# A linear-attention and mixture-of-experts kernel: 240 token places an expert, and another sequence first

## The chip, the cores and the metric

The kernel runs on one core of a Trainium2 chip. A core has a matrix engine (TensorE, PE in the profile; its weight loads are PEld), a vector engine (VectorE, DVE), a scalar engine (ScalarE, ACT), a general one (GpSimd, POOL) and a queue engine that here only issues transfers (SyncE, SP). They run side by side and wait for one another by semaphores; 16 DMA engines move data. The metric is the device time of one execution in microseconds, less is better.

## The reference

Two stages, float32, shapes r, k, v, w [4 sequences, 8 heads, 768 places, 48]. The first is a recurrence along each sequence, the second sends half of the 3072 rows to one of 8 experts each:

```python
for t in range(S):                                   # per batch and head
    cur = einsum('bhd,bhe->bhde', u[None] * k[t], v[t])
    y[t] = einsum('bhd,bhde->bhe', r[t], state + cur)
    state = w[t][..., None] * state + einsum('bhd,bhe->bhde', k[t], v[t])
x = y.transpose(0, 2, 1, 3).reshape(3072, 384)
out = x.copy()
xc = x[x @ w_skip > 0]
e_idx = argmax(xc @ w_gate, axis=1)
gate = softmax(xc @ w_gate) at e_idx
out[those rows] = xc + gate * (relu(xc @ w1[e_idx]) @ w2[e_idx])   # w1 [384, 1024], w2 [1024, 384]
```

## The kernel before

**Attention stage.** The work is 24 chunks: `seq` (line 64) lists them, sequence after sequence, six chunks of 128 places each. The order on every engine is written out by hand (the loop at line 672, under a manual schedule): step s computes the outputs of chunk s, the scores of chunk s + 1 and the preparation of chunk s + 2. A chunk has one tile `wrk` with w, r and k for all heads: 96 of its 128 partitions hold the two halves of the heads (16 to 111), the others hold whatever lies beside them in memory and are masked out by `rowsk`, one number a partition. Three such tiles go round.

Preparation of a chunk: VectorE scans w into q (`prep_scan`, line 309), GpSimd multiplies r by k into rk (`bonus_keys`, 318), GpSimd multiplies k by q into kq (326), VectorE scans w into rh (331), and rp = r times rh (336) is made by GpSimd, for the first chunk by VectorE. TensorE: `scores` (358, from kq and rp), `bonus_sums` (377, from rk), `rows_of_keys` (348, transposes of kq, which ScalarE copies to kt, 350), `update` (390, from kt and v), `outputs` (409, 413), `rows_out` (425). VectorE masks the scores (364) and multiplies the bonus sums by the turned v (`bonus`, 381); ScalarE evicts.

SyncE issues the loads in the order of the program: `load_chunk` (167), `load_turned` (163) and `load_v` (182). The first chunk has nothing before it in memory, so only its 96 rows are loaded (173, 174), into a tile that GpSimd and VectorE have cleared before (240, 243). `setup` (245) also clears other tiles and lets TensorE multiply zeros: `fill` (663) issues that many matmuls of 512 columns, 11 at the start, 4 in step -1 (729) and 3 in step 0 (702).

Between the chunks a router gives each token an expert and a rank within it. Tokens whose rank is beyond the capacity `CAP` (31) set a flag, upon which a slow general path computes everything again (940); it isn't run here.

**Expert stage.** Each expert has CAP = 256 token places, in two tiles of 128, gathered by an indirect DMA from the output (`gather`, 439). The expert weights and tokens are split into a high and a low part of a reduced 32-bit type (fp32r in the profile), and three products are added. For each of eight pieces q of the hidden layer, nine matmuls go into one bank (882 to 884; weights stationary, 256 tokens moving). ScalarE takes the relu as its high part hh (889), VectorE the low part hl (894). Then, for each token tile j, 24 matmuls (906 to 908; hidden values stationary, 384 columns of w2 moving), VectorE adds the gated result (915), and GpSimd scatters the rows back (820). Between the two products, `tokens` (809) transposes the tokens of the next expert (815). The splitting of the next expert's weights (88, 89) runs beside the matmuls. Expert 0 is worked differently: its first tile is done ahead, in the holes at the end of the attention stage, and its tiles keep 128 places.

## Time and profile before

| what | value |
|---|---|
| median of 3 runs | 286.65 us (286.0 to 287.15) |
| the profiled execution | 286.06 us in all, span of its instructions 284.2 us |
| TensorE busy | 95% of the span |
| VectorE, ScalarE, GpSimd busy | 76%, 56%, 51% |
| attention stage | up to about 133 us |
| experts 1 to 7 | from about 156 us to the end |

The span is from the first to the last instruction; the execution has some 1.9 us more around it. Busy time of TensorE is no measure of how close it is to its peak: matmuls are pipelined, each shows a duration that overlaps the next one's, and what one costs in a stream is the distance from its start to the next start. L882 is line 882 of the kernel. Engine names with a q (SPq, ACTq) are the engines' issue queues. "x8" is a count.

### The profile page before, as it was taken

To read this page: it belongs to the slowest core of one execution; us is meant where nothing else is said; L and a number is where in the kernel's file an instruction comes from. 1 tells how busy PE (TensorE), PEld (TensorE's weight loads), DVE (VectorE), ACT (ScalarE), POOL (GpSimd) and SP (SyncE) were. 2 spreads that over 40 slices of the span, in tenths; PEclk is the share of its full clock that TensorE was granted. 3 is DMA by queue.
4 is the path that set the end of the run, shared out by engine and by line. 5 is a ranking of instruction groups with operands and counts; after the bars stand their busy time and mean duration, and the time that the engine had idled before them with its cause. 6 is when DMAs were issued, how large, how long until landed. Compare 5 with 4: busy or idle time off the path is not lost.

```text
span 284.2 us, 8967 instructions
## 1 busy us (share of the span) xinstructions
PE 271.2 (95%) x3601; PEld 248.9 (88%) x3602; DVE 217.0 (76%) x414; ACT 159.4 (56%) x464; POOL 145.9 (51%) x140
## 2 busy tenths in 40 slices
PE   6998999999999999999999999999999999999993
PEld 2687878788887888887999999999999999999992
DVE  7997999999989999972747697948859588595320
ACT  5175555787658957768416573827638276381310
POOL 4986775699978998974656625011030110201111
PEclk9999999999999999999999999999999999999999
DMA  7999999998999869992078997565672656700001
GB/s 217 239 311 333 277 345 339 363 332 246 297 278 302 252 218 348 308 310 65 28 256 294 345 314 267 212 213 200 221 258 68 231 200 221 268 5 28 10 5 41
DMA packets 26131, 64.41 MB, mean 227 GB/s; under 512 B 4342, under 2 KB 15386, under 8 KB 26080
## 3 DMA queue, kind: packets, MB, share of 16 engines
q1 hardware_dynamic: 23712, 58.14, 62.3%
q0 software_dynamic: 2048, 5.48, 5.9%
q8 instruction: 30, 0.49, 0.7%
q10 hardware_dynamic: 320, 0.13, 0.2%
q14 instruction: 21, 0.17, 0.2%
HBM read 56.69 MB, written 7.86 MB: 227 GB/s over the span
## 4 chain that ended last, share of the span: by engine, by line
PE 57%; POOL 8%; issue 6%; DVE 4%; ACT 3%; DMA 1%; POOLq 0%; DVEq 0%; ACTq 0%
PE psH L884 7%; PE psH L883 7%; PE psH L882 7%; PE psO L906 6%; PE psO L908 6%; PE psO L907 6%; PE psH L133 4%; PE psY L409 3%; POOL rp L336 2%; PE psA L358 2%; POOL kq L326 2%; PE psY L413 2%; PE psX L815 2%; PE psO L658 2%; PE psX L425 1%
## 5 line engine op out<-in xcount | busy, mean ns | idle before, releaser
L820 POOL DMA_INDIRECT out<-fin,ids x16 | 16.8, 1047 | 99.1 <-DVE fin L915 92.7
L889 ACT ACTIVATE hh<-psH 128x256 fp32r<-128x256 f32 x60 | 23.1, 385 | 56.6 <-PE psH L884 53.4
L884 PE MATMUL psH<-xTh,w1l 128*128 128x256 f32 x168 | 47.5, 283 | 0.0
L883 PE MATMUL psH<-xTl,w1h 128*128 128x256 f32 x168 | 47.5, 283 | 0.0
L882 PE MATMUL psH<-xTh,w1h 128*128 128x256 f32 x168 | 47.5, 283 | 0.0
L906 PE MATMUL psO<-w2h,hh 128*128 128x384 f32 x120 | 40.9, 341 | 0.0
L908 PE MATMUL psO<-w2h,hl 128*128 128x384 f32 x120 | 40.2, 335 | 0.0
L907 PE MATMUL psO<-w2l,hh 128*128 128x384 f32 x120 | 40.1, 335 | 0.0
L894 DVE SCALAR_TENSOR_TENSOR hl<-psH,hh 128x256 fp32r<-128x256 f32 x60 | 25.1, 418 | 13.3 <-ACT hh L889 12.0
L326 POOL TENSOR_TENSOR kq<-wrk,q 128x512 f32<-128x512 f32 x24 | 28.2, 1177 | 11.7 <-DVE q L309 3.5
L364 DVE TENSOR_TENSOR asb<-psA,c_sb 128x512 f32<-128x512 f32 x48 | 30.4, 676 | 3.5 <-PE psA L358 3.4
L331 DVE TENSOR_TENSOR_SCAN rh<-wrk,rowsk,pss 128x520 f32<-128x520 f32 x24 | 31.1, 1296 | 2.0
L318 POOL TENSOR_TENSOR rk<-wrk 128x512 f32<-128x512 f32 x24 | 31.0, 1292 | 2.4 <-DMA wrk<-wrk 2.4
L884 PEld LDWEIGHTS psH<-xTh,w1l 128*128 128x128 f32 x168 | 32.2, 192 | 0.0
L883 PEld LDWEIGHTS psH<-xTl,w1h 128*128 128x128 f32 x168 | 32.2, 192 | 0.0
L882 PEld LDWEIGHTS psH<-xTh,w1h 128*128 128x128 f32 x168 | 32.2, 191 | 0.0
L309 DVE TENSOR_TENSOR_SCAN q<-wrk,pss 128x520 f32<-128x520 f32 x24 | 29.5, 1230 | 3.0 <-DMA wrk<-wrk 0.9
L336 POOL TENSOR_TENSOR rp<-wrk,rh 128x512 f32<-128x512 f32 x23 | 27.2, 1181 | 5.4 <-DVE rh L331 5.0
L89 DVE TENSOR_TENSOR w2l<-r,w2h 128x512 fp32r<-128x512 f32 x42 | 27.7, 685 | 2.0 <-ACT w2h L88 1.4
L409 PE MATMUL psY<-asb,v 128*48 128x128 f32 x384 | 26.5, 276 | 2.6 <-DVE psY L381 2.3
L915 DVE SCALAR_TENSOR_TENSOR fin<-psO,gates,xg 128x384 f32<-128x384 f32 x15 | 9.3, 618 | 25.2 <-PE psO L908 24.6
L358 PE MATMUL psA<-rp,kq 64*64 64x128 f32 (+1 forms) x768 | 26.0, 251 | 1.8 <-issue 1.1
(154 smaller groups left out, 608.4 us busy)
## 6 DMA issues: line engine op xcount, KB each, us to landing
r<-w SPq DMA_DIRECT2D x48, 512.0 KB
wrk<-wrk SPq DMA_DIRECT2D x21, 772.5 KB
v<-vN SPq DMA_DIRECT2D x24, 192.0 KB
vt<-wrk SPq DMA_DIRECT2D x48, 96.0 KB
out<-x SPq DMA_DIRECT2D x24, 192.0 KB
wrk<-wrk SPq DMA_DIRECT2D x1, 579.4 KB
wrk<-wrk SPq DMA_DIRECT2D x1, 512.0 KB
wrk<-wrk SPq DMA_DIRECT2D x1, 384.0 KB
```

The costliest lines, as they stand in the source:

```text
L318: nc.gpsimd.tensor_tensor(work[i]["rk"].rearrange("p a j -> p (a j)"), t[:, R_OFF:K_OFF], t[:, K_OFF:V_OFF], op=ALU.mult)
L326: nc.gpsimd.tensor_tensor(kq, wk["k"], wk["q"][:, :, 1:1 + P], op=ALU.mult)
L331: nc.vector.tensor_tensor_scan(rh.rearrange("p a j -> p (a j)"), wk["w"][:, 0:NP * CW], reads_at[:, :NP * CW], rowsk, op0=ALU.mult, op1=AL ...
L336: eng.tensor_tensor(rp, wk["r"], rh[:, :, :P], op=ALU.mult)
L358: nc.tensor.matmul(psa[g][j:j + HP, a, j:], wk["kq"][rows, a, j:j + HP], wk["rp"][rows, a, j:], start=True, stop=True)
L409: nc.tensor.matmul(y_at(a, g), v[:, 2 * a + g], wk["asb"][g][:, a], start=False, stop=True, skip_group_check=True)
L882: nc.tensor.matmul(ps, w1h[:, o:o + P], xTh[:, kc], start=(kc == 0), stop=False)
L883: nc.tensor.matmul(ps, w1h[:, o:o + P], xTl[:, kc], start=False, stop=False)
L884: nc.tensor.matmul(ps, w1l[:, o:o + P], xTh[:, kc], start=False, stop=(kc == KC - 1))
L906: nc.tensor.matmul(pso, h[j, fc][0], w2h[:, o], start=(fc == 0), stop=False)
L907: nc.tensor.matmul(pso, h[j, fc][0], w2l[:, o], start=False, stop=False)
L908: nc.tensor.matmul(pso, h[j, fc][1], w2h[:, o], start=False, stop=(fc == FC - 1))
```

## The change

Three things. `CAP` is 240: the second token tile of experts 1 to 7 has 112 rows, the moving tile of lines 882 to 884 has 240 columns, and gather, transposes, scatter and the last addition take 112 rows in the second tile. Expert 0 keeps its shapes. The order of the sequences is 1, 0, 2, 3; chunk numbers in memory come from a list `chunk`, and since the first chunk processed now has rows before it in memory, it is loaded with 128 rows, and nothing is cleared for it. In the set-up the loads of the first three chunks come first on SyncE, ahead of the turned v and v of the first; `rowsk` is made by four memsets; four clears move from step -2 to the set-up. GpSimd makes rp of the first chunk too, and for the first two chunks rk is made behind rp. The fillers are 2 in step -1 and none in step 0.

```diff
-CAP = 256
+CAP = 240
...
-    seq = [(b, c) for b in range(B) for c in range(NC)]
+    seq = [(b, c) for b in (1, 0, *range(2, B)) for c in range(NC)]
+    chunk = [b * NC + c for b, c in seq]
...
         def load_chunk(i):
             b, c = seq[i]
             rows = wrk.rearrange("b c g d n -> (b c g d) n")
-            at = 2 * D * i
+            at = 2 * D * chunk[i]
             t = wrk_sb[i % NBUF]
-            if i == 0:
-                nc.sync.dma_start(t[KO:LO, :R_OFF], rows[:2 * D, :R_OFF])
-                nc.sync.dma_start(t[KO:LO, R_OFF:V_OFF], rows[:2 * D, R_OFF:V_OFF])
-                nc.scalar.dma_start(c_sb[:, :C_IOTA], cst[:, :C_IOTA])
-                shifted(nc.scalar, u_sb, uP)
-                return
-            to, at = (t, at - KO) if i < n - 1 else (t[KO:LO], at)
-            for cs in (slice(0, R_OFF), slice(R_OFF, V_OFF)) if i == 1 else (slice(0, V_OFF),):
+            to, at = (t, at - KO) if 0 < chunk[i] < n - 1 else (t[KO:LO], at)
+            for cs in (slice(0, R_OFF), slice(R_OFF, V_OFF)) if i < 2 else (slice(0, V_OFF),):
                 nc.sync.dma_start(to[:, cs], rows[at:at + to.shape[0], cs])
 
         def load_v(i):
...
 
         count_w = scratch(1)
 
-        def clear_w(eng, i):
-            eng.memset(wrk_sb[i][:, :R_OFF], 1.0)
-
-        def clear_rk(eng, i):
-            eng.memset(wrk_sb[i][:, R_OFF:], 0.0)
-
         def setup():
-            clear_w(nc.gpsimd, 0)
-            nc.gpsimd.memset(vt_sb[0], 0.0)
-            clear_rk(nc.vector, 0)
-            load_chunk(0)
+            for i in range(3):
+                load_chunk(i)
+            for t in vt_sb[:3]:
+                nc.gpsimd.memset(t, 0.0)
+            load_turned(0)
+            load_v(0)
+            nc.scalar.dma_start(c_sb[:, :C_IOTA], cst[:, :C_IOTA])
+            shifted(nc.scalar, u_sb, uP)
+            nc.gpsimd.memset(wgp_sb, 0.0)
+            nc.gpsimd.memset(vt_sb[3], 0.0)
+            nc.gpsimd.memset(onesb, 1.0)
+            nc.gpsimd.memset(ohs, 0.0)
+            nc.gpsimd.memset(key, 0.5)
             nc.vector.memset(warm, 0.0)
-            load_chunk(1)
-            nc.gpsimd.memset(vt_sb[1], 0.0)
-            load_v(0)
-            load_turned(0)
             nc.vector.memset(pss, 0.0)
             ints = ones_w.bitcast(U32)
             for a in range(NP):
 ...
-            nc.vector.tensor_reduce(rowsk, ident[:, KO:LO], axis=AX, op=ALU.add)
+            nc.vector.memset(rowsk, 1.0)
+            nc.vector.memset(rowsk[:KO], 0.0)
+            nc.vector.memset(rowsk[96:], 0.0)
+            nc.vector.memset(rowsk[96:LO], 1.0)
             nc.vector.tensor_scalar(reads_w.bitcast(U32), ints, rowsk, None, op0=ALU.mult)
             nc.scalar.activation(junk0, warm[:, 0:1], AF.Exp)
             for z in psa:
                 nc.scalar.copy(z.rearrange("p a j -> p (a j)"), warm)
-            nc.gpsimd.memset(vt_sb[2], 0.0)
-            nc.gpsimd.memset(wgp_sb, 0.0)
             for o in range(2):
                 eye = ident[half(o, D), HP * o:HP * o + D]
                 for g in range(2):
...
-            if i > 0:
+            if i > 1:
...
-            eng = nc.gpsimd if i > 0 else nc.vector
-            eng.tensor_tensor(rp, wk["r"], rh[:, :, :P], op=ALU.mult)
+            nc.gpsimd.tensor_tensor(rp, wk["r"], rh[:, :, :P], op=ALU.mult)
+            if i < 2:
+                bonus_keys(i)
...
-            nc.sync.dma_start(out[i * P:(i + 1) * P], x.rearrange("p o i d -> p (o i d)"))
+            nc.sync.dma_start(out[chunk[i] * P:(chunk[i] + 1) * P], x.rearrange("p o i d -> p (o i d)"))
+
+        def width(j):
+            return min(P, CAP - j * P)
...
         def gather(s, pool):
...
+            w = width(s % 2) if s > 1 else P
-                out=xg[s], out_offset=None, in_=out,
-                in_offset=bass.IndirectOffsetOnAxis(ap=idr[:, s % 2, s // 2:s // 2 + 1], axis=0),
+                out=xg[s][:w], out_offset=None, in_=out,
+                in_offset=bass.IndirectOffsetOnAxis(ap=idr[:w, s % 2, s // 2:s // 2 + 1], axis=0),
...
-                if s + 4 < n:
+                if 3 <= s + 4 < n:
...
-                    if s == 0:
-                        fill(3)
...
-                if s == -2:
-                    bonus_keys(0)
-                    nc.gpsimd.memset(vt_sb[3], 0.0)
-                    nc.gpsimd.memset(onesb, 1.0)
-                    nc.gpsimd.memset(ohs, 0.0)
-                    nc.gpsimd.memset(key, 0.5)
...
-                        fill(4)
+                        fill(2)
...
             xTh = moe.tile([P, KC, CAP], F32R, tag="xTh", name=f"xTh{e}")
             xTl = moe.tile([P, KC, CAP], F32R, tag="xTl", name=f"xTl{e}")
             for j in range(2):
+                w, ts = width(j), slice(j * P, j * P + width(j))
                 ps = ps1.tile([P, KC, P], F32, tag="psT", name=f"psX2{e}_{j}", bufs=2)
                 for kc in range(KC):
-                    nc.tensor.transpose(ps[:, kc], xg[2 * e + j][:, kc * P:(kc + 1) * P], ident)
-                split(xTh[:, :, j * P:(j + 1) * P], xTl[:, :, j * P:(j + 1) * P], ps)
+                    nc.tensor.transpose(ps[:, kc, :w], xg[2 * e + j][:w, kc * P:(kc + 1) * P],
+                                        ident[:w, :w])
+                split(xTh[:, :, ts], xTl[:, :, ts], ps[:, :, :w])
             xTs[e] = xTh, xTl
 
         def scatter(s, o):
+            w = width(s % 2)
             sc = nc.gpsimd.indirect_dma_start(
-                out=out, out_offset=bass.IndirectOffsetOnAxis(ap=ids[:, s % 2, s // 2:s // 2 + 1],
+                out=out, out_offset=bass.IndirectOffsetOnAxis(ap=ids[:w, s % 2, s // 2:s // 2 + 1],
                                                                axis=0),
-                in_=o, in_offset=None, bounds_check=NT - 1, oob_is_err=False)
+                in_=o[:w], in_offset=None, bounds_check=NT - 1, oob_is_err=False)
             tc.declare_no_dep(sc.ins, group="rows", reason="tokens are scattered to rows of their own")
             tc.add_to_no_dep_group("rows", sc.ins)
 
...
 
             h = {}
             nh = FC if e > 0 else FC // 2
+            n_ = CAP if e > 0 else 2 * P
             for q in range(nh):
                 ps = (ps1 if q % 4 < 2 else ps2).tile(
-                    [P, CAP], F32, tag=("psA0", "psA1", "psY", "psB")[q % 4], name=f"psH{e}_{q}")
-                hh = moe.tile([P, CAP], F32R, tag="hh", name=f"hh{e}_{q}", bufs=NHB)
-                hl = moe.tile([P, CAP], F32R, tag="hl", name=f"hl{e}_{q}", bufs=NHB)
+                    [P, n_], F32, tag=("psA0", "psA1", "psY", "psB")[q % 4], name=f"psH{e}_{q}")
+                hh = moe.tile([P, 2 * P], F32R, tag="hh", name=f"hh{e}_{q}", bufs=NHB)[:, :n_]
+                hl = moe.tile([P, 2 * P], F32R, tag="hl", name=f"hl{e}_{q}", bufs=NHB)[:, :n_]
                 if e == 0:
                     for i in range(2):
                         ts = slice(i * P, (i + 1) * P)
...
-                        ts = slice(j * P, (j + 1) * P)
+                        ts = slice(j * P, j * P + width(j))
...
             w2h, w2l = wsp[e, 2], wsp[e, 3]
             for j in range(1 if e == 0 else 0, 2):
                 pso = ps1.tile([P, DM], F32, tag=("psu", "pss")[j], name=f"psO{e}_{j}")
+                w = width(j) if e > 0 else P
+                po = pso[:w]
                 for fc in range(FC):
                     o = slice(fc * DM, (fc + 1) * DM)
-                    nc.tensor.matmul(pso, h[j, fc][0], w2h[:, o], start=(fc == 0), stop=False)
-                    nc.tensor.matmul(pso, h[j, fc][0], w2l[:, o], start=False, stop=False)
-                    nc.tensor.matmul(pso, h[j, fc][1], w2h[:, o], start=False,
+                    nc.tensor.matmul(po, h[j, fc][0], w2h[:, o], start=(fc == 0), stop=False)
+                    nc.tensor.matmul(po, h[j, fc][0], w2l[:, o], start=False, stop=False)
+                    nc.tensor.matmul(po, h[j, fc][1], w2h[:, o], start=False,
                                      stop=(fc == FC - 1))
                 more(2)
                 if j == 0 and e in (1, 2):
                     (row_tests, verdict)[e - 1]()
                 s = 2 * e + j
                 o = moe.tile([P, DM], F32, tag="fin", name=f"fin{e}_{j}", bufs=3)
-                nc.vector.scalar_tensor_tensor(o, pso, gates[:, j, e:e + 1], xg[s],
+                nc.vector.scalar_tensor_tensor(o[:w], po, gates[:w, j, e:e + 1], xg[s][:w],
                                                op0=ALU.mult, op1=ALU.add)
                 if later_pairs:
                     first.append((s, o))
```

## Rows read from the trace of the kernel before

**Rows 1.** The page: engine table (busy, share, instructions) and the chain by line.
```profile
PE 271.2 (95%) x3601; PEld 248.9 (88%) x3602; DVE 217.0 (76%) x414; ACT 159.4 (56%) x464; POOL 145.9 (51%) x140
...
PE psH L884 7%; PE psH L883 7%; PE psH L882 7%; PE psO L906 6%; PE psO L908 6%; PE psO L907 6%; PE psH L133 4%; PE psY L409 3%; POOL rp L336 2%; PE psA L358 2%; POOL kq L326 2%; PE psY L413 2%; PE psX L815 2%; PE psO L658 2%; PE psX L425 1%
```

**Rows 2.** Timeline of the first product: start us, duration us, engine, line, operation, tiles, count.
```profile
196.00 0.28 PE L882 MATMUL psH<-xTh,w1h 128*128 128x256 f32 x1
196.00 0.19 PEld L883 LDWEIGHTS psH<-xTl,w1h 128*128 128x128 f32 x1
...
199.96 0.28 PE L882 MATMUL psH<-xTh,w1h 128*128 128x256 f32 x1
```

**Rows 3.** Timeline of the second product.
```profile
203.09 0.33 PE L906 MATMUL psO<-w2h,hh 128*128 128x384 f32 x1
...
205.17 0.33 PE L906 MATMUL psO<-w2h,hh 128*128 128x384 f32 x1
```

**Rows 4.** The chain in order of time: start us, us, engine, tile, line, count.
```profile
146.01 5.36 PE psH L133 x48
...
235.75 0.66 PE psX L815 x6
...
253.38 0.66 PE psX L815 x6
```

**Rows 5.** Stretches: length, then busy us (instructions) by engine, clock, DMA share, GB/s.
```profile
8.00:13.80 5.80, 5.48 (x94) 3.74 (x99) 5.73 (x8) 0.78 (x3) 5.80 (x9) 1.00 0.94 230
13.80:18.90 5.10, 5.10 (x120) 4.58 (x122) 4.74 (x9) 3.25 (x11) 4.68 (x5) 1.00 0.93 306
...
40.00:60.00 20.00, 19.57 (x402) 16.75 (x397) 18.72 (x36) 12.74 (x47) 14.12 (x13) 1.00 1.04 347
```

**Rows 6.** Timeline of the start, all engines; in brackets idle time and its releaser.
```profile
0.74 0.39 ACTq L175 DMA_DIRECT2D c_sb<-cst  x1
...
1.96 0.32 SPq L174 DMA_DIRECT2D wrk<-wrk  x1
...
3.30 4.56 PE L666 MATMUL psw<-warm 128*128 128x512 bf16 x11
...
6.40 1.17 POOL L326 TENSOR_TENSOR kq<-wrk,q 128x512 f32<-128x512 f32 x1 [3.37 <-DMA wrk<-wrk]
...
6.82 1.30 DVE L336 TENSOR_TENSOR rp<-wrk,rh 128x512 f32<-128x512 f32 x1
...
7.53 1.72 POOL L318 TENSOR_TENSOR rk<-wrk 128x512 f32<-128x512 f32 x1
...
8.27 1.09 PE L358 MATMUL psA<-rp,kq 64*64 64x128 f32 x32 [0.40 <-DVE rp L336]
...
10.58 0.59 ACT L350 COPY kt<-psT 128x512 f32<-128x512 f32 x1 [3.40 <-PE psT L348]
...
11.34 0.67 PE L390 MATMUL psu<-v,kt 128*64 128x48 f32 x16
...
11.94 0.82 PE L666 MATMUL psw<-warm 128*128 128x512 bf16 x3
...
12.69 1.08 PE L409 MATMUL psY<-asb,v 128*48 128x128 f32 x16
...
13.70 0.98 PE L358 MATMUL psA<-rp,kq 64*64 64x128 f32 x28
```

**Rows 7.** Timeline at the switch from the transposes to the second product: weight loads.
```profile
165.21 0.19 PEld L906 LDWEIGHTS psO<-w2h,hh 128*128 128x128 f32 x1
...
165.32 0.19 PEld L907 LDWEIGHTS psO<-w2l,hh 128*128 128x128 f32 x1
```

**Rows 8.** The page's costliest groups, two of VectorE: busy us, mean ns, idle before, releaser.
```profile
L894 DVE SCALAR_TENSOR_TENSOR hl<-psH,hh 128x256 fp32r<-128x256 f32 x60 | 25.1, 418 | 13.3 <-ACT hh L889 12.0
...
L89 DVE TENSOR_TENSOR w2l<-r,w2h 128x512 fp32r<-128x512 f32 x42 | 27.7, 685 | 2.0 <-ACT w2h L88 1.4
```

**Rows 9.** Timeline of the end, GpSimd.
```profile
280.26 0.98 POOL L820 DMA_INDIRECT out<-fin,ids  x1 [3.18 <-DVE fin L915]
```

More of the change, by code (lines that the diff above doesn't have):

```diff
@@ L502, in low_vals @@
                 if not last:
-                    nc.scalar.copy(vals[:, :, :2, 0], tok[:, i0:i0 + m])
+                    nc.scalar.copy(vals[:, :, :2, 0], tok[:, chunk[i0]:chunk[i0] + m])
                 nc.scalar.copy(vals[:, :, 2], gate)
```

## The prediction

> **What bounds the kernel now.** I read the page's table of engines and its chain first: TensorE is busy for 95% of the span, and the chain names the expert matmuls of lines 882 to 884 and 906 to 908 before all else [rows 1]. Then the timeline of the expert stage, from one matmul start to the next, since a busy share says little of pipelined matmuls. In the first product of an expert, 33 matmuls of 256 columns lie between the starts 196.00 and 199.96, 120.0 ns each [rows 2]; in the second product 12 matmuls of 384 columns lie between 203.09 and 205.17, 173.3 ns each [rows 3]. The stream has no hole: an expert takes 253.38 - 235.75 = 17.63 us [rows 4], and 72 x 0.120 + 6 transposes (0.66) + 48 x 0.1733 = 8.64 + 0.66 + 8.32 = 17.62. So in this stage a nanosecond off each matmul start comes off the end.
>
> In the attention stage TensorE is the pacer too. After the scores of the second chunk processed (13.70) it is busy for all of 5.10 us, and for 19.57 of 20 us in the middle of the stage [rows 5]. Before that it isn't: it starts its scores at 8.27, waits for data between short bursts, and begins its unbroken stream with the outputs of the first chunk at 12.69 [rows 6]. So the first 13 us are worth what they move that 12.69, no more.
>
> **Capacity 240, the expert matmuls.** For experts 1 to 7 lines 882 to 884 issue 7 x 8 x 9 = 504 matmuls, whose moving tile shrinks from 256 to 240 columns. The two pitches are 128 columns and 53.3 ns apart, which is 0.4167 ns a column (the 2.4 GHz level) and leaves 13.3 ns a matmul that doesn't depend on columns. On that line 240 columns cost 100 + 13.3 = 113.3 ns, a gain of 6.67 ns, and 504 x 6.67 ns = 3.36 us. No row shows a matmul of this reduced type under 256 columns, so the value is bounded from both sides. The bound on the gain is that line. The bound on the other side is that the weight load, which still has 128 columns, takes over. Each load starts as the matmul before it starts [rows 2], and streams with less moving work show how fast loads can follow each other: 48 f32 matmul passes of 128 columns in 5.36 us, 112 ns each; 6 transposes in 0.66 us, 110 ns [rows 4]. Where the second product begins behind the transposes, a weight load of the reduced type at 165.21 is followed by the next at 165.32 [rows 7], so it too fits in 110 ns. All three lie below 113.3, so I take the line, and keep 0 to 3.36 us for the range.
>
> [...]
>
> The rest of this part is small. In the second product the second tile has 112 weight columns, but its time goes with the 384 moving ones: nothing. The transposes run at a weight load's pace (110 ns) and their loads keep 128 columns: nothing, at most 21 x 13 ns. ScalarE's and VectorE's evictions (lines 889 and 894) get shorter, but wait for TensorE; on VectorE an eviction (0.42) and a low part of the next expert's weights (0.69) [rows 8] make 1.1 us beside 1.02 us of matmuls for each of the eight hidden pieces, a lag of under 1 us, which the second product absorbs since it uses those pieces in order over 4 us. The gathers are hidden. The last scatter is not: issued at 280.26, it ends the span at 284.2 [rows 9]. With 112 of 128 rows it gains between nothing and an eighth of 3.9 us; I take 0.1, since issue and latency hardly go with rows.
>
> **The start: what goes.** GpSimd's clearing of w and VectorE's clearing of r and k go. They hold back the first loads: that of r and k is issued at 1.96 [rows 6], behind that of w. Without them SyncE can begin at about 0.7 (ScalarE's first load stands at 0.74) and issue r and k behind w at 1.1, 0.85 earlier. What comes: both loads have 128 rows, a third more bytes. Which of the two wins is read from the first GpSimd multiply: kq waited for that DMA until 6.40, 4.4 us after its issue. Bounds: landing as long after issue as before, 5.5; or longer in the ratio of bytes, 1.1 + 4.4 x 4/3 = 6.95. In between I take 6.3, their middle, 0.1 before. Call it L.
>
> **The start: rp on GpSimd.** Before, VectorE made rp (6.82 to 8.12) beside kq, and GpSimd went on to rk, which ended at 9.25. Now GpSimd makes kq, rp and rk in a row, each of the same size, some 1.2 us: the scores can start at L + 2.4 (before 6.40 + 1.87), and rk ends at L + 3.6 (before 6.40 + 2.85). Behind rk come the bonus sums, the transposes and ScalarE's kt, which ended 1.92 after rk (11.17 behind 9.25), and the update, 0.67: outputs at L + 3.6 + 1.9 + 0.8 = L + 6.3. Before, the outputs stood 12.69 - 6.40 = 6.29 behind that landing, because VectorE's rp, the next chunk's scan, its masks and its bonus product came one after the other. The half microsecond and more that GpSimd adds is thus what VectorE gives back, and the outputs move as L does: -0.9 to +0.55, taken as -0.1. Queued behind rp on GpSimd are rk, then kq and rp of the second chunk, ready at L + 6.0 and wanted, behind the outputs, at L + 7.3 (13.70 before): no wait. Moving four small clears from between the chunks to the set-up costs nothing; they end by 4 us, GpSimd's idle time.
>
> **The start: the queue.** Chunk 2's load (772 KB) now passes v and the turned v of the first chunk on SyncE. Those 0.39 MB are wanted at 11.3 (the update) and a little later. By the shapes in the code, 2.9 MB must land by then: from 1.7 us on at the 306 GB/s of the stretch after 13.8, 11.2, just in time; at the 230 GB/s of the stretch before it [rows 5], 14.3, and with the update behind it the outputs at 15.0, 2.3 us late. I take the first, because the queue is full earlier now and the second stretch holds small transfers and waits for issue; 2.3 stays as a bound. Earlier chunk loads later on are worth nothing by themselves, as TensorE paces there. The fillers that go (3 of line 702, 2 of line 729) ran while TensorE waited for VectorE or ScalarE; cost nothing, as long as the real work keeps the clock. [...]
>
> **Sum.** -3.36 (matmuls) - 0.1 (tail) - 0.1 (start) = -3.56. The profiled execution has 284.2 us of span and 286.06 us in all; that would become 282.5. The median of the runs is 0.59 above it, so 283.1 there; I say 283.0.
>
> **The rivals.** First: the weight load is the bound at 240 columns and the pitch stays near 120. [...] Against it: the 110 ns of [rows 7] and the 110 to 112 ns of [rows 4]. It gives 286.65 - 0.2 = 286.4.
>
> Second, on the other side: a moving tile under 256 columns loses the reduced type's single-pass rate and runs at the pace of the f32 passes. Two passes of 112 ns for 128 columns are 1.75 ns a column, 420 ns for 240; 504 x 0.30 us = +151, about 437 us. It decides as soon as the pitch passes 120 + 3.56/504, about 127 ns. For it: no row shows the type under 256 columns. Against it: the exact line through 256 and 384 with 2.4 GHz, which shows no sign of a step.
>
> Third: the start eats most of it. [...]
>
> Fourth: the change doesn't fit its data. More than 240 tokens for one expert would set the flag that runs the slow general path. Counting the reference's own choice gives 234 at most, so I give it 1 in 100.
>
> **How the numbers follow.** Forecast 0.76. Its own range is 281.4 to 284.8: at the low end the start gains 0.9 + 0.8 more than I take for it and for waits inside the stage; at the high end a matmul gains only 5 ns (0.84 us less) and the start loses 0.9. First rival 0.10, second 0.05, third 0.08, fourth 0.01. The range 281.2 to 285.8 holds the forecast and the milder half of the third, some 0.80, and leaves out the first, the second, the fourth and the rest of the third. A change of 0.5%, about what a measurement of this kernel can tell from none, ends at 285.2 and 288.1. Faster: the forecast and a little of the third, 0.77. Slower: the second, the fourth and a bad end of the third, 0.07. The rest, 0.16, within it.
>
> **What would show it.** In the changed trace: starts of lines 882 to 884 113 ns apart (rival one: 118 to 120; two: far above); an expert's period 17.63 - 0.48 = 17.15 us; the first kq at about 6.3, the scores at 8.7, rk behind rp, the outputs at 12.6 and no idle TensorE after; the first bonus product not waiting for a DMA. I am wrong if the pitch isn't on the line, or if the outputs stand later than 13.3.

## The result, and the profile of the changed kernel

The changed kernel takes 283.23 us (median of 14 executions, 282.47 to 290.28) where the kernel before takes 286.55 beside it. The ratio is 0.989, with a 95% interval of 0.987 to 0.991; it leaves out 290.28, the one execution that lies more than 1.5% above the fastest. The forecast was 283.0. The profiled execution takes 283.2 us with a span of 281.4 (before 286.06 and 284.2), so the spans differ by 2.8 us.

The page's engine table and its three groups of the first product (columns: busy us, mean ns, idle before):

```profile
PE 265.0 (94%) x3596; PEld 244.1 (87%) x3597; DVE 214.0 (76%) x415; ACT 159.1 (57%) x464; POOL 147.1 (52%) x140
...
L879 PE MATMUL psH<-xTl,w1h 128*128 128x240 f32 x168 | 46.3, 275 | 0.0
L878 PE MATMUL psH<-xTh,w1h 128*128 128x240 f32 x168 | 46.1, 275 | 0.0
L880 PE MATMUL psH<-xTh,w1l 128*128 128x240 f32 x168 | 46.1, 274 | 0.0
```

TensorE is still the engine that bounds the kernel; its busy time fell by 6.2 us [rows 1]. The matmuls are read from start to start. TensorE's timeline: one expert's first product from its first matmul to its last and the transposes behind it, then the first product of a later expert and the start of the one after:

```profile
191.28 0.27 PE L878 MATMUL psH<-xTh,w1h 128*128 128x240 f32 x1
191.39 0.28 PE L879 MATMUL psH<-xTl,w1h 128*128 128x240 f32 x1
...
199.25 0.28 PE L880 MATMUL psH<-xTh,w1l 128*128 128x240 f32 x1
199.36 0.78 PE L808 MATMUL psX<-c_sb,xg 128*128 128x128 f32 x6
199.91 0.42 PE L904 MATMUL psO<-w2h,hh 128*128 128x384 f32 x1
...
225.41 0.28 PE L878 MATMUL psH<-xTh,w1h 128*128 128x240 f32 x1
...
233.40 0.28 PE L880 MATMUL psH<-xTh,w1l 128*128 128x240 f32 x1
...
242.48 0.27 PE L878 MATMUL psH<-xTh,w1h 128*128 128x240 f32 x1
```

The same product before, first and last matmul:

```profile
191.69 0.28 PE L882 MATMUL psH<-xTh,w1h 128*128 128x256 f32 x1
...
200.20 0.29 PE L884 MATMUL psH<-xTh,w1l 128*128 128x256 f32 x1
```

From the first start to the last there are 71 steps. Before, they take 8.507 us in this product, which is 119.8 ns each (the 33 steps of [rows 2] gave 120.0), and as much within 1 ns in the six others. Changed, they take 7.99 to 8.00 us in six of the seven first products (225.41 to 233.40 is one), 112.5 ns each; that at 191.28 is the shortest, 112.2. An expert's period is 242.48 - 225.41 = 17.07 us, 0.56 less than in [rows 4]. The pitch is 72 x 7.3 ns = 0.53 of that, and the six transposes, from their first start to what follows them, take 0.550 us instead of 0.573.

The timeline of the start, all engines (brackets: idle time and what ended it), to be held against [rows 6]:

```profile
0.73 3.58 SPq L175 DMA_DIRECT2D wrk<-wrk  x5
...
5.40 1.17 POOL L321 TENSOR_TENSOR kq<-wrk,q 128x512 f32<-128x512 f32 x1 [2.10 <-DVE wrk L319]
...
6.77 1.18 POOL L330 TENSOR_TENSOR rp<-wrk,rh 128x512 f32<-128x512 f32 x1 [0.19 <-DVE rh L326]
...
7.85 4.14 SPq L678 DMA_DIRECT2D wgp_sb<-wgp  x4
...
8.00 1.09 PE L354 MATMUL psA<-rp,kq 64*64 64x128 f32 x32 [1.39 <-POOL rp L330]
...
11.79 0.58 PE L386 MATMUL psu<-v,kt 128*64 128x48 f32 x15 [1.10 <-DMA v<-vN]
...
12.11 0.52 SPq L175 DMA_DIRECT2D wrk<-wrk  x1
...
12.26 1.04 PE L405 MATMUL psY<-asb,v 128*48 128x128 f32 x15
...
13.23 1.09 PE L354 MATMUL psA<-rp,kq 64*64 64x128 f32 x32
...
18.18 1.24 DVE L304 TENSOR_TENSOR_SCAN q<-wrk,pss 128x520 f32<-128x520 f32 x1 [1.90 <-DMA wrk<-wrk]
```

The first kq comes 1.0 us earlier than before, and it waits for VectorE, no longer for its load. The outputs (12.26) and the scores of the second chunk (13.23) come about 0.45 earlier. The update waits 1.1 us for v. Then the scan of the fourth chunk (chunk 3) waits 1.90 us for its load, which was issued at 12.11.

Three stretches of this execution (length, busy us of each engine with instructions, granted clock, DMA share, GB/s), the same as in [rows 5]:

```profile
8.00:13.80 5.80, 4.56 (x109) 3.69 (x114) 5.26 (x8) 1.25 (x4) 5.80 (x5) 1.00 0.89 209
13.80:18.90 5.10, 5.10 (x124) 4.63 (x118) 3.18 (x5) 3.36 (x13) 3.08 (x4) 1.00 0.94 296
40.00:60.00 20.00, 18.21 (x375) 15.75 (x371) 18.21 (x36) 12.23 (x46) 14.12 (x13) 1.00 1.03 343
```

TensorE is busy for 18.21 us of the 20 from 40 to 60, where it was 19.57. Part of that is three idle pieces that end on nothing the profile shows ("issue"); such pieces stand at other places in other executions. The view of TensorE's waits from 36 to 62 (us in total, times, longest):

```profile
PE psY L373 <- issue: 0.7, 1, 0.7
PE psT L344 <- issue: 0.6, 1, 0.6
PE psA L354 <- issue: 0.5, 1, 0.5
```

Four marks on the timeline split every profiled execution into the same stretches: ScalarE's copy of the last chunk's xT (the outputs, on their way to the rows), the first matmul of expert 1's first product, the start of the last matmul of the second product, and the end. The first two rows give the same copy of the first chunk (chunk 0) and of the fifth (chunk 4). "Again" is a second profile of the unchanged changed kernel; the others are the experiments below.

| us | before | capacity only | start only | changed | again | v first | start late |
|---|---|---|---|---|---|---|---|
| copy of xT, chunk 0 | 13.82 | 13.98 | 13.32 | 13.34 | 14.24 | 12.88 | 14.96 |
| copy of xT, chunk 4 | 35.21 | 37.66 | 34.86 | 35.07 | 35.11 | 33.98 | 35.66 |
| 24 chunks | 132.72 | 135.19 | 133.83 | 133.49 | 133.07 | 132.14 | 133.18 |
| to expert 1 | 23.31 | 23.30 | 23.32 | 23.29 | 23.30 | 23.31 | 23.29 |
| experts 1 to 7 | 122.96 | 119.02 | 125.25 | 119.03 | 119.02 | 119.02 | 119.03 |
| last matmul to end | 5.21 | 5.59 | 5.20 | 5.59 | 5.41 | 5.43 | 6.50 |
| span | 284.2 | 283.1 | 287.6 | 281.4 | 280.8 | 279.9 | 282.0 |

The row of experts 1 to 7 is the gain: -3.93 us. The row of the 24 chunks is where executions differ, by up to 3 us, with either start and with either capacity.

### The profile page after: what moved, and what is told of

Same layout as the page of the kernel before. It is cut to its first block, busy times and chain, and to the rows that moved or that the text cites. A ratio compares the mean times of both kernels' runs of the same rounds, so it can differ in the third digit from the quotient of the medians.

```text
span 281.4 us, 8960 instructions
## 1 busy us (share of the span) xinstructions
PE 265.0 (94%) x3596; PEld 244.1 (87%) x3597; DVE 214.0 (76%) x415; ACT 159.1 (57%) x464; POOL 147.1 (52%) x140
## 4 chain that ended last, share of the span: by engine, by line
issue 36%; PE 31%; POOL 15%; DVE 8%; DMA 5%; ACT 2%; POOLq 1%; SPq 1%; DVEq 0%; ACTq 0%
PE psY L405 5%; POOL out L815 5%; DMA wrk<-wrk 4%; PE psH L134 4%; PE psA L354 4%; PE psX L421 3%; POOL rp L330 3%; PE psY L409 3%; POOL kq L321 2%; PE psY L373 2%; DVE asb L360 2%; PE psT L344 2%; POOL hot L530 2%; DVE psY L377 2%; PE psO L658 2%
## 5 line engine op out<-in xcount | busy, mean ns | idle before, releaser
L885 ACT ACTIVATE hh<-psH 128x240 fp32r<-128x240 f32 (+1 forms) x60 | 22.4, 373 | 52.9 <-PE psH L880 45.6
L879 PE MATMUL psH<-xTl,w1h 128*128 128x240 f32 x168 | 46.3, 275 | 0.0
L878 PE MATMUL psH<-xTh,w1h 128*128 128x240 f32 x168 | 46.1, 275 | 0.0
L880 PE MATMUL psH<-xTh,w1l 128*128 128x240 f32 x168 | 46.1, 274 | 0.0
L904 PE MATMUL psO<-w2h,hh 128*128 128x384 f32 (+1 forms) x120 | 40.9, 341 | 0.0
L906 PE MATMUL psO<-w2h,hl 128*128 128x384 f32 (+1 forms) x120 | 40.3, 336 | 0.0
L905 PE MATMUL psO<-w2l,hh 128*128 128x384 f32 (+1 forms) x120 | 40.2, 335 | 0.0
L890 DVE SCALAR_TENSOR_TENSOR hl<-psH,hh 128x240 fp32r<-128x240 f32 (+1 forms) x60 | 24.3, 404 | 12.8 <-ACT hh L885 6.6
L330 POOL TENSOR_TENSOR rp<-wrk,rh 128x512 f32<-128x512 f32 x24 | 28.5, 1188 | 5.7 <-DVE rh L326 5.3
L414 ACT COPY xT<-psY 128x512 f32<-128x512 f32 x24 | 14.1, 586 | 24.2 <-PE psY L409 17.7
```

What stands on the lines that cost most here:

```text
L330: nc.gpsimd.tensor_tensor(rp, wk["r"], rh[:, :, :P], op=ALU.mult)
L878: nc.tensor.matmul(ps, w1h[:, o:o + P], xTh[:, kc], start=(kc == 0), stop=False)
L879: nc.tensor.matmul(ps, w1h[:, o:o + P], xTl[:, kc], start=False, stop=False)
L880: nc.tensor.matmul(ps, w1l[:, o:o + P], xTh[:, kc], start=False, stop=(kc == KC - 1))
L904: nc.tensor.matmul(po, h[j, fc][0], w2h[:, o], start=(fc == 0), stop=False)
L905: nc.tensor.matmul(po, h[j, fc][0], w2l[:, o], start=False, stop=False)
```

## The experiments

Each ratio is against the kernel before, measured beside that experiment; its medians, with the one above, were 286.55 to 287.69 us, so times of experiments that were not beside each other compare no better than that.

**The capacity alone.** The kernel before with the 240 places, the second tile narrowed as in the diff ahead, and nothing else of the change:

```
-CAP = 256
+CAP = 240
```

> The kernel before with the capacity of 240 alone. Theory: the whole of the change's gain is the expert matmuls, whose starts went from 119.8 to 112.5 ns apart, and the new start gives nothing in the end; then this kernel takes 286.6 - 504 x 7.3 ns = 282.9 us (282.6 to 283.2), ratio 0.987, with an expert's period of 17.1 us. Rival: the start gives half a microsecond of the change's 3.2; then this kernel takes 283.5 to 283.8.

Measured: 283.65 us (6 executions, 282.5 to 285.11), ratio 0.990 with an interval of 0.987 to 0.992. Its experts 1 to 7 take 119.02 us, as in the changed kernel. The capacity alone gives what the whole change gives, within the interval. The time lies above the theory's range and in the rival's; the interval is 1.6 us wide and holds both, so this run alone doesn't decide about half a microsecond of the start.

**The start alone.** The changed kernel with 256 places again (one line):

```
-CAP = 240
+CAP = 256
```

> The changed kernel with the capacity put back to 256, so the new start alone. Theory: the outputs of the first chunk stand at about 12.2 instead of 12.69, but chunk 3's load lands as late as in the changed kernel (scan of chunk 3 waits about 1.9 us for it) and the gain is gone by the fifth chunk; 286.3 to 287.2 us, no difference. Rival: the gain at the first outputs passes through to the end, 286.0 or less.

Measured: 287.4 us (12 executions, 286.08 to 289.9), ratio 1.002 with an interval of 0.998 to 1.006: nothing that can be told from no change. In its profile TensorE waited 2.0 us once, in the first product of expert 1, for VectorE's low part. That is its longer row of experts 1 to 7, and no other profile in the table has that wait. So the new start changes the time by -0.5 to +1.6 us, which leaves the rival of a gain of half a microsecond at its very edge, and the 24 chunks of the profiles (133.83 with it, 132.72 without) don't speak for a gain either.

**Is it the columns or the weight load that sets 112 ns?** First 192 places, which is 48 columns fewer; tokens of a rank of 192 or more in their expert are left out of the products.

```
-CAP = 256
+CAP = 192
```

> The kernel before with 192 places an expert for experts 1 to 7 (64 rows in the second tile); tokens of a rank of 192 or more within their expert are left out of the expert products, and the start is that of before. Theory (columns set the pitch until the 128-column weight load does): the line through 256 and 240 columns, 0.4167 ns a column, gives 112.5 - 20 = 92.5 ns at 192, which is less than the 108 to 112 ns of the nearest weight loads, so the pitch of lines 880 to 884 should stop at 108 to 112 ns; the expert part (from the last xT eviction to the end) 147.9 - 504 x 0 to 4.5 ns = 145.7 to 147.9 us, the time 281.3 to 283.6. Rival A (no floor, columns alone): pitch 92.5, 504 x 20 = 10 us less than with 240, expert part 137.9, time 273.5. Rival B (a narrow tile loses the single pass below some width under 240): pitch far above 120, time above 300.

Measured: 283.87 us (4 executions, 283.17 to 285.68), ratio 0.989 (0.983 to 0.995), nothing gained over 240. TensorE's timeline of one first product:

```profile
191.92 0.25 PE L890 MATMUL psH<-xTh,w1h 128*128 128x192 f32 x1
...
199.83 0.28 PE L892 MATMUL psH<-xTh,w1l 128*128 128x192 f32 x1
199.94 0.82 PE L820 MATMUL psX<-c_sb,xg 128*128 128x128 f32 x6
200.69 0.44 PE L916 MATMUL psO<-w2h,hh 128*128 128x384 f32 x1
```

(199.83 - 191.92) / 71 = 111.4 ns. On a line of columns it would be 92. Fewer columns than 240 give back 1.1 ns a matmul and no more. The rest of an expert even got longer: the six transposes take 0.75 us instead of 0.55, with waits between them, and its period is 17.20 instead of 17.07.

Then the same kernel with the middle three of nine matmuls loading 64 weight columns; half of their partial products is left out.

```
+hp, oh = (ps, o + P) if kc != 1 else (ps[:P // 2], o + P // 2)
-nc.tensor.matmul(ps, w1h[:, o:o + P], xTh[:, kc], ...)
+nc.tensor.matmul(hp, w1h[:, o:oh], xTh[:, kc], ...)
```

> As cap192, but the middle three of the nine matmuls of each hidden piece load 64 weight columns instead of 128 and fill half of the piece; the other half of those partial products is left out. Theory (cap192's pitch of 111.4 ns is the load of 128 weight columns): behind a matmul whose successor loads only 64 columns the start comes on the line of the moving columns, some 92.5 ns, so the mean pitch of lines 890 to 893 falls from 111.4 to about (6 x 111.4 + 3 x 92.5) / 9 = 105 ns. Rival (a fixed time for each matmul of this type, whatever it loads): all of them stay at 111.4 ns.

TensorE's timeline, at the beginning and the end of one first product (PEld are weight loads, two of which are shown; 128*64 are the narrow ones):

```profile
191.31 0.25 PE L891 MATMUL psH<-xTh,w1h 128*128 128x192 f32 x1
...
191.42 0.19 PEld L893 LDWEIGHTS psH<-xTh,w1l 128*128 128x128 f32 x1
191.51 0.27 PE L893 MATMUL psH<-xTh,w1l 128*128 128x192 f32 x1
...
191.53 0.14 PEld L891 LDWEIGHTS psH<-xTh,w1h 128*64 128x64 f32 x1
191.62 0.25 PE L891 MATMUL psH<-xTh,w1h 128*64 128x192 f32 x1
191.71 0.25 PE L892 MATMUL psH<-xTl,w1h 128*64 128x192 f32 x1
191.80 0.25 PE L893 MATMUL psH<-xTh,w1l 128*64 128x192 f32 x1
191.89 0.27 PE L891 MATMUL psH<-xTh,w1h 128*128 128x192 f32 x1
...
198.65 0.28 PE L893 MATMUL psH<-xTh,w1l 128*128 128x192 f32 x1
198.76 0.38 PE L820 MATMUL psX<-c_sb,xg 128*128 128x128 f32 x2
```

Measured: 280.52 us (one execution), and 72 matmuls from 191.31 to 198.76, a mean of 103.5 ns. The three narrow ones take 0.27 us here (191.62 to 191.89) and 2.10 us for all 24, which is 87.5 ns each; the other 48 take 111.5. The loads themselves last 0.19 us with 128 columns and 0.14 with 64. So there is no fixed time per matmul, and the 192 moving columns, which are the same for both kinds, don't set the 111.4 ns: the load of 128 weight columns does. The mean came out as the theory had it, the place did not: a step is short behind a matmul that itself loaded 64 columns, and the step from the last wide one to the first narrow one (191.51 to 191.62) is still 0.11 us, since the narrow load begins only 0.11 us after the wide load before it (191.42 to 191.53). The narrow matmuls also fill 64 instead of 128 rows of their output, and no run separates that from the load.

**v ahead of chunk 2's load.** The update of the first chunk waited 1.1 us for v. The changed kernel with the load of chunk 2 behind the turned v and v of the first chunk:

```
-for i in range(3):
+for i in range(2):
     load_chunk(i)
 ...
 load_v(0)
+load_chunk(2)
```

> The changed kernel with the turned v and v of the first chunk issued ahead of chunk 2's load again. Theory: in the changed kernel the update of the first chunk waits 1.1 us for v; here it doesn't, the outputs stand at 11.5 to 11.7 instead of 12.2, but chunk 3's load still lands at about 18 and takes the gain back: 283.0 to 283.3 us. Rival: what the outputs win comes off the end, 282.5 to 282.7.

Measured: 283.59 us (8 executions, 281.71 to 285.47), ratio 0.991 with an interval of 0.987 to 0.994. In its profile the update no longer waits for v, the outputs stand at 11.81 and the first xT copy at 12.88, 0.46 earlier than in the changed kernel; chunk 3's scan still waits 1.57 us for its load. The profiled execution is the fastest of the eight (281.71), and chunk 4's xT copy in it is 1.09 earlier than in the changed kernel, so there the gain was not taken back. The median shows no gain; it lies above the ranges of both theories, and an interval of 2 us can't tell them apart.

**The small loads behind chunk 3's.** In the changed kernel line 678 holds SyncE from 7.85 to 11.99 with four transfers of 4.5 KB, ahead of chunk 3's load. Not all of that is issuing; SyncE's longest wait in the first 20 us (us in total, times, longest):

```profile
SPq L678 <- DMA wrk<-wrk: 1.5, 1, 1.5
```

The changed kernel with those four behind chunk 3's load:

```
+if 3 <= s + 4 < n:
+    load_chunk(s + 4)
+if on(s + 3) and s + 3 >= 1:
+    load_turned(s + 3)
+    load_v(s + 3)
 if s == -1:
     (the four loads of wgp)
-(the same five lines)
```

> The changed kernel with the four small loads of the router's weights issued behind chunk 3's loads instead of ahead of them. Theory: chunk 3's load stands behind them on SyncE; issued at about 9.5 instead of 12.1 it lands by 16, the scan of chunk 3 no longer waits 1.9 us, and the first chunks keep their half microsecond or more: 282.3 to 282.8 us. Rival: the transfers and TensorE's own stalls of the stage take the time anyway, 283.0 to 283.4; or the small loads, now late, hold up the first rows out (line 421), up to 283.7.

Measured: 288.27 us (9 executions, 285.12 to 292.55), slower than the changed kernel by 4 us (by the ratios) to 5 (by the medians) and level with the one before (1.003, interval 0.999 to 1.007). Chunk 3's load was indeed issued at 9.61, but now the first row outputs wait for wgp. TensorE's timeline of that wait, then two stretches of the same execution:

```profile
18.76 2.01 PE L421 MATMUL psX<-wgp_sb,xT 128*128 128x105 f32 x8 [2.42 <-DMA wgp_sb<-wgp]
20.70 0.98 PE L386 MATMUL psu<-v,kt 128*64 128x48 f32 x15
```

```profile
14.00:18.00 4.00, 2.34 (x58) 1.73 (x53) 3.82 (x5) 2.69 (x9) 3.82 (x4) 1.00 0.76 156
18.00:22.00 4.00, 3.24 (x29) 3.08 (x31) 1.89 (x3) 0.57 (x2) 2.36 (x2) 0.57 1.03 349
22.00:26.00 4.00, 4.00 (x77) 3.64 (x75) 0.05 (x1) 1.32 (x4) 0.00 (x0) 0.58 1.06 337
```

TensorE idled for 2.42 us, and in the two stretches that hold the end of that wait and the work behind it its granted clock was 0.57 and 0.58: the eight matmuls took 2.01 us there, 1.04 us in the profile of v first. From the first chunk's xT copy (14.33) to the second's (24.60) it took 10.3 us, in the changed kernel 5.0. A wait of 2.4 us cost 5.3 in this execution: the 5.84 us from 18.76 to 24.60 are 3.16 in the changed kernel (15.18 to 18.34), where the granted clock from 13.80 to 18.90 was 1.00, so 2.7 of the 5.3 came behind the wait. The one execution of the nine with a mean granted clock of 1.0 took 285.12, the others, at 0.977 to 0.990, 285.8 to 292.6. That an earlier load of chunk 3 would pay, whatever it passes, fell.

**The small loads on ScalarE's queue.** To have both, v first and no hold on SyncE:

```
-nc.sync.dma_start(wgp_half[...], wgp[...])
+nc.scalar.dma_start(wgp_half[...], wgp[...])
```

(and the edit of v first).

> The changed kernel with two transfers moved: v and the turned v of the first chunk ahead of chunk 2's load (as in v_first), and the four small loads of line 678 issued by ScalarE instead of SyncE, so that SyncE isn't held for 2.7 to 4.1 us ahead of chunk 3's load. Theory (SyncE's hold is what makes the fourth chunk's scan wait): chunk 3's load is issued at 9.3 to 10 instead of 11.6 to 12.1, the scan of chunk 3 starts without its 1.6 to 2.0 us of waiting for a DMA, TensorE doesn't wait near 22.9, time 0.5 to 1.5 us under v_first in like executions: 282.0 to 283.0. Rival (those waits are absorbed later, since the DMA rate and TensorE set the stage): the time stays within 0.5 us of 283.4. Another way: four issues in a row on ScalarE (some 2.7 us) hold up kt at 10.5 and with it the update: outputs later than 12.3, time 283.5 to 285.

Measured: 283.71 us (12 executions, 281.84 to 291.94), ratio 0.986 (0.983 to 0.989). Chunk 3's load was issued at 13.49, later than in the changed kernel, and its scan still waited 1.79 us. The outputs stood at 13.35, as late as the third way has it, but not for its reason: kt waited for TensorE's transposes (ScalarE idled 3.63 us ahead of it), at a granted clock of 0.61 from 10 to 14 us, and not for ScalarE. SyncE's longest wait in the first 20 us (us in total, times, longest):

```profile
SPq L175 <- DMA wgp_sb<-wgp: 4.0, 1, 4.0
```

SyncE waited 4.0 us for the small transfers to land, though ScalarE had issued them. So what stands ahead of chunk 3's load is more than the issuing. Why a transfer on SyncE waits for one that ScalarE issued isn't shown. The forecast that this edit frees chunk 3's load fell; whether an earlier issue would pay, it could not test.

**The fillers.** The same kernel, and the changed kernel itself, with the fillers of before:

```
-fill(2)
+fill(4)
 ...
 update(s)
+if s == 0:
+    fill(3)
```

> As wgp_act, with the fillers of before again (four instead of two behind the rows of keys of the first chunk, three behind its update). Theory (the few filler matmuls that went cost nothing): median within 0.4 us of wgp_act. Rival (with fewer fillers TensorE's granted clock falls near the start in some executions; the executions of the changed kernel lie between 282.5 at 0.998 and 290.3 at 0.984): the executions of this kernel all have a mean clock of 0.99 or more, and its highest time lies within 1% of its lowest, while those of wgp_act spread wider; the fillers themselves may cost up to 0.6 us.

> The changed kernel with the fillers of before (four instead of two behind the rows of keys of the first chunk, three behind its update). Theory (fillers only fill waiting time): median within 0.5 us of the changed kernel. What it is to tell apart: if the long executions of the changed kernel (286.6 and 290.3 of 14) come from a lower granted clock at the start, none of this one should lie over 1% above its lowest, while the changed kernel again has some; if they come from elsewhere, both have them alike.

Measured: 283.88 us (6 executions, 282.24 to 284.24) and 283.45 us (6 executions, 282.74 to 285.14). The ratios are 0.987 (0.983 to 0.992) and 0.988 (0.984 to 0.993). The first lies 0.2 us above the kernel without the fillers beside it (0.9 if that one's three long executions are left out), the second 0.8 above the changed kernel's second set beside it (below), more than the 0.5 of its theory; six executions each don't tell that from nothing. Whether the fillers prevent the long executions stays open. The signs of the rival were there: with them the clocks are 0.991 or more and no execution is 1% over its lowest, without them three of the twelve are. But none of six beside three of twelve can be chance, and the changed kernel's second set had none either. The lower clock at the start they do not prevent. Two stretches of the changed kernel with them (the changed kernel's own first profile has 1.00 here):

```profile
7.00:10.00 3.00, 1.74 (x40) 1.74 (x44) 2.56 (x3) 0.55 (x3) 2.97 (x3) 0.75 1.02 358
10.00:14.00 4.00, 4.00 (x43) 2.42 (x36) 3.42 (x6) 0.78 (x3) 4.00 (x4) 0.76 0.87 152
```

**rp of the first chunk back on VectorE.**

```
-nc.gpsimd.tensor_tensor(rp, ...)
+eng = nc.gpsimd if i > 0 else nc.vector
+eng.tensor_tensor(rp, ...)
```

> The changed kernel with the first chunk's rp back on VectorE. Theory (rp on GpSimd costs nothing, since the update then waits for v, which sits behind chunk 2's load): rk 1.2 us earlier (ends near 8.0), the bonus sums, transposes and kt about 1.2 earlier, but the update still waits for v until about 11.8; outputs at 12.2 +- 0.2, scores of the second chunk 13.2 to 14.0 (VectorE's next scan is 1.2 later), time 283.2 +- 0.8. Rival (rp on GpSimd held up the outputs): outputs at 11.3 or less, first xT eviction before 12.6, time 282.5 or less.

Measured: 283.05 us (4 executions, 282.27 to 283.94), ratio 0.986 (0.981 to 0.992). Its outputs came at 13.32, 1.06 later than in the changed kernel, and so outside of what either theory gave; the granted clock was 0.81 between 7 and 10 us and 0.72 between 10 and 14, where the changed kernel's first profile has 1.00. So the run doesn't tell what rp on GpSimd costs. The loss was gone by chunk 4: chunk 3's scan (17.25) waited for nothing, and the copy of chunk 4's xT stood at 35.13, against 35.07.

**The changed kernel again, and its start made late.** The second has eight more clears of an unused buffer on GpSimd ahead of the first kq, and 16 instead of 11 fillers.

```
 nc.gpsimd.memset(key, 0.5)
+for _ in range(8):
+    nc.gpsimd.memset(vt_sb[3], 0.0)
```

> The changed kernel once more, unchanged, on the chip of the two runs beside it. Theory: 283.2 +- 0.6 as median; a part of its executions (about one in seven before) over 1% above the lowest. Another profile also tells which of its stalls in the attention stage (1.9 us at the scan of chunk 3, then 0.5 to 0.7 us each near 44.5, 50.8 and 57.5) come back: those that belong to the schedule should, those of one execution should not.

> The changed kernel with eight more clears of an unused buffer on GpSimd ahead of the first chunk's kq (3.9 us of GpSimd, so kq starts about 1.8 us later) and 16 instead of 11 fillers before the scores, so that TensorE's clock has no more reason to fall. Theory, formed on the earlier runs (the first outputs don't set the end: the scan of chunk 3 waits for its load in any case, and first evictions between 12.9 and 14.5 led to the same 132 to 134 at chunk 23): first xT eviction 1.2 to 1.8 later, chunk 4's eviction at most 0.5 later, time within 0.5 us of the changed kernel on this chip. Rival, the reading of the prediction (the start is worth what it moves the first outputs): time 1.2 to 1.8 us above the changed kernel.

Measured: again 282.65 us (6 executions, 281.57 to 283.46), ratio 0.984 (0.980 to 0.988); start late 285.61 (12 executions, 283.42 to 287.83), ratio 0.992 (0.989 to 0.996). Of the stalls of the first profile, that at chunk 3's scan wasn't there again, nor were the three between 36 and 62 (another of that kind, 0.9 us, stood at 120.6); they belonged to one execution. What was there is a lower clock at the first scores. Two stretches of the second profile of the changed kernel, and the scan that waited before:

```profile
7.00:10.00 3.00, 1.68 (x36) 1.68 (x38) 2.62 (x4) 0.55 (x3) 3.00 (x4) 0.71 1.02 357
10.00:14.00 4.00, 3.76 (x58) 2.83 (x50) 3.45 (x6) 0.78 (x3) 4.00 (x4) 0.79 0.77 143
```

```profile
17.10 1.24 DVE L304 TENSOR_TENSOR_SCAN q<-wrk,pss 128x520 f32<-128x520 f32 x1
...
35.11 0.59 ACT L414 COPY xT<-psY 128x512 f32<-128x512 f32 x1 [1.40 <-PE psY L409]
```

The outputs came 0.9 us later (13.17) than in the first profile, of which 0.5 are the first kq's (5.94, behind its load), and chunk 4's xT copy within 0.04 (35.11 against 35.07): what clock and load took here, the wait for chunk 3's load took there. The start made late doesn't follow this. Its kq stands at 7.88, 1.9 later than in the profile beside it, and its outputs at 13.88. It costs 2.96 us over the run beside it, more than the rival's 1.2 to 1.8, so neither theory gives its size. Its profile, at 283.81, is one of its three fastest and doesn't hold the loss: its chunks end at 133.18, like the others, and 1.1 us lie behind its last matmul. The granted clock in it is 1.00 from 7 to 14 us; whether the five more fillers did that isn't shown. Its three executions with a mean granted clock of 0.994 to 0.996 take 283.4 to 284.5, its nine with 0.987 to 0.991 take 284.9 to 287.8. So the clock goes with the loss; in which stretch it fell in those nine, no profile shows.

## Why the forecast held, step by step

**The matmuls.** -3.36 was forecast, with 113.3 ns; the pitch went from 119.8 to 112.5, and experts 1 to 7 give -3.93. 504 x 7.3 ns = 3.68 of that are the matmuls. The prediction's 2.4 GHz is the inverse of its 0.4167 ns a column, which is 53.3 / 128 ns by [rows 2] and [rows 3]; the profiles give the clock as a share, not in GHz. The term was 0.3 too small, just outside of its bound, because [rows 2] and [rows 3] were joined by a line with a constant of 13.3 ns. That constant isn't one: it is 13.1 at 256 columns, 12.5 at 240, and 87.5 - 80 = 7.5 ns at 192 with a narrow load. The line gave a size close to the truth, not the mechanism; why the 16 columns gave 7.3 ns and not 6.7 isn't shown. Of the other 0.25, 0.14 are the transposes (six times 0.573 - 0.550), which were taken as nothing, at most 0.27; the rest is spread over the stage.

**Rival 1, the weight load.** Its mechanism exists and its place was missed: the floor is 111.4 ns, not 120. The prediction's own bound, 110 to 112 ns by [rows 4] and [rows 7], had put it there, but only [rows 7] shows loads of this type. That the transposes, 110 ns apart, run at a weight load's pace isn't borne out. Three transposes of the run with 192 places load 128 columns of 64 rows, within 0.26 us:

```profile
200.36 0.26 PEld L820 LDWEIGHTS psX<-c_sb,xg 64*128 64x128 f32 x3 [0.17 <-issue]
```

These loads begin 0.06 us apart (their matmuls move 64 columns; no run parts that from the rows), so 110 ns is not what a load of 128 columns takes in every case, and the transposes' pace was no safe measure of the floor. At 240 columns the pitch stands 1.1 ns above the floor, so the change takes nearly all that fewer columns can give.

**Rival 2, no single pass under 256 columns.** The line through 256 and 384 columns could not speak against it, since two pitches always lie on one. The runs do: 240 columns start 0.8 ns under the line, 192 at the pace of the load (111.4 ns), and 192 with a narrow load at 87.5 ns.

**The tail.** -0.1 was forecast, 0 to 0.5 of gain. It is a loss: from the last matmul to the end 5.41 and 5.59 us in the two profiles, 5.21 before; the last scatter was issued at 277.08 and took 4.3 us to the end, 3.9 in [rows 9].

```profile
277.08 0.95 POOL L815 DMA_INDIRECT out<-fin,ids  x1 [3.17 <-DVE fin L913]
```

Both profiles with 256 places have 5.2, those with 240 have 5.4 to 6.5, and the two with 192 have 5.3 and 5.5. Why fewer rows should take longer isn't shown. That issue and latency hardly go with rows was the author's estimate; no run parts them from the rest of the 4.3 us.

**The start.** L was taken as 6.3 between 5.5 and 6.95. kq came at 5.40 and waited for VectorE, not for the load; in the second profile it waited for the load until 5.94. So the landing is at or below the lower bound in the one, inside in the other, and the third more bytes cost less than was taken. The outputs came 6.9 us behind kq instead of 6.3, because the update waits 1.1 us for v, half of the 2.3 that was kept as a bound. Without that wait, in v first, they are the 6.3 (5.52 to 11.81). Net, the first outputs gained 0.45 in the first profile, where 0.1 was taken, and lost 0.5 in the second.

**What the first outputs are worth.** "The first 13 us are worth what they move that 12.69, no more" doesn't hold as a rule, though the sum hardly shows it. In three executions (the changed kernel twice, and with rp on VectorE) the outputs stood at 12.26, 13.17 and 13.32, and chunk 4's xT copies at 35.07, 35.11 and 35.13. What 1 us at the start gave was gone by then. In the first of them chunk 3's scan waited 1.9 us for a load that SyncE could issue only behind the four small transfers, and TensorE 1.2 us behind it (the prediction had no idle TensorE there); in the other two the scan was that much later and waited for nothing.

```profile
22.87 1.08 PE L405 MATMUL psY<-asb,v 128*48 128x128 f32 x16 [1.19 <-DVE psY L377]
```

These three are no rule either: by the table, 0.46 won at the first copy in v first was 1.09 at chunk 4, and 1.62 lost in start late was 0.59. What chunk 4's copy wins does count: from there to the last chunk's copy seven of the fourteen profiles take 97.51 to 97.58 us, the others up to 1.5 more (2.7 in the run with the small loads late). The forecast had called earlier loads worth nothing since TensorE paces there; up to chunk 4 a load can pace instead.

**The lower clock.** The author's estimate for a lower clock at the first scores was +1.5 us; no run shows that term. In the second profile of the changed kernel the granted clock was 0.71 from 7 to 10 us and 0.79 from 10 to 14, the outputs came 0.9 later (0.5 of it by the load), and the execution was no slower (282.71 against 283.2). At another place, behind a wait that ended at 18.76, the same work took 2.7 us more (5.84 against 3.16), at a granted clock of 0.57 and 0.58. So not only the length of slow work counted in these executions, but where it fell.

**The sum.** Forecast -3.56, measured -3.3 by the medians beside each other: -3.93 for experts 1 to 7, +0.2 to +0.4 for the tail, and the rest, about +0.3, is chunks of the attention stage that vary from one execution to the next by more than that. The main term was right in its mechanism and near in size; that the sum came within 0.3 is partly luck, since the expert stage gave 0.6 more than forecast and tail and chunks took as much back.

## What to carry to other kernels

Trim the moving columns of a weight-changing matmul until the 128-column load sets the pitch (111.4 ns here), and stop: the load's own pace stands in the trace where loads of the same type follow each other with little moving work (110 ns in [rows 7]). A stall removed at the start was worth nothing here that a median could tell, while a later transfer was late in any case; look down the same queue for it, and at what the queue itself waits for (4.0 us in one profile here), before costing the start. A new wait of TensorE may cost more than its length: one of 2.42 us cost 5.3 here, with a granted clock of 0.57 and 0.58 around its end and behind it.

## What the runs showed of the hardware that was not expected

A matmul of this reduced type with 192 moving columns takes, from its start to the next, 111.4 ns with 128 weight columns and 87.5 ns with 64. Behind an idle time of 2.42 us TensorE's granted clock was 0.57 and 0.58 in two stretches of 4 us, though it was busy throughout the second. The length of the idle time alone doesn't tell: in start late TensorE was busy for 0.67 of the 3 us from 7 to 10, ahead of the first scores, and the granted clock there and from 10 to 14 was 1.00. A scatter of 112 rows ended 0.2 to 0.4 us later behind the last matmul than one of 128, in one profile 1.3.
